# Attention and two feed-forward layers on one core: source order in the rounds, four slices decoded ahead, masks by the third unit

## The chip, the cores and the metric

One core of a Trainium2 chip runs the whole program. The metric is the device time of one execution in microseconds (us). TensorE (PE) multiplies, VectorE (DVE), ScalarE (ACT) and GpSimd (POOL) do the rest, SyncE (SP) issues nearly all loads and stores. Each engine works through its own queue in order and waits on semaphores of the others.

## What is computed

Sliding-window attention over 2 batches, 8 heads, 768 positions, head size 64 (window 128, 4 sink keys), then two feed-forward layers on the 1536 tokens of 512 values, with 2048 hidden values each:

```
scores = scale * q @ k.T, masked to (sink or window)
x = softmax(scores) @ v             -> 1536 x 512
g = where(h > 0, h, exp(min(h, 0)) - 1),  h = x @ w_in ;  x = g @ w_out
g = max(h, 0) + alpha * min(h, 0),        h = x @ w_in2 ; out = g @ w_out2
```

The weights arrive as 64-bit floating point numbers, and the kernel takes them apart itself on the chip.

## The kernel before

**Three products for one.** Every feed-forward product is made of three matmuls (`matmul3`, L287): each operand is split into a rounded part (wh, gh, xh) and a residual (wl, gl, xl).

**Decoding.** A half slice is 128 x 512 weights: slice fc of the first (io=0) or second matrix (io=1) of layer m. `load_w` (L192) brings its raw words over SP's queue. `decode_w` (L257) takes it apart in four phases, between which its caller can put other work: two activations on ScalarE (L266, L267), four steps on VectorE (L269 to L278), the cast wh on ScalarE (L282), the subtraction wl (L284) on VectorE, or on the engine that the caller names.

**Attention.** 32 units of one or two blocks of 110 queries, for two heads at a time. A loop over steps s (L610) runs three units at once: scores of unit s (L510, then per tile a fused mask and minimum on VectorE, L518, and an exponential on ScalarE, L523), the sums and their reciprocals (L533, L536) with the normalising on GpSimd (L540), the transposes of the probabilities of unit s-1 (L554) with copies out of PSUM (L638), and the product with the values of unit s-2 (L575), whose result is rounded on ScalarE (xh, L583) and its residual taken on VectorE (xl, L585). Masks are made on VectorE by `make_mask` (L454): blocks 0 and 1 ahead of the loop, 2, 3 and 4 at the end of steps 0, 1 and 5, from index ramps that GpSimd made at the start.

**Round 0 inside the attention.** While the attention runs, TensorE takes pieces of the first layer's round 0 as fill (L591): a round is four slices of hidden values, `g1` makes one slice's hidden values for a stretch of tokens, `g2` adds four slices' product to one quarter of the output. Where there is no fill, small matmuls keep TensorE busy (L246). The eight half slices of round 0 are decoded in steps 0 to 7, the first four with the subtraction on VectorE, the others on GpSimd. In this part (from L597) each engine's instructions stand in the order of the source.

**After a piece** (`after`, L316 and L353): for `g1` of layer 0 ScalarE's relu and exp (L321, L322), VectorE's combining step (L323), ScalarE's rounding copy gh (L335) and GpSimd's residual gl (L336); in the text this is the gate. For `g2` one copy (L355) or addition (L357). A PSUM slot (four of them) comes free when VectorE's or ScalarE's last read of it is done.

**The rounds.** The last stretch of round 0's tokens (328 columns, "the first item" in the text) and rounds 1 to 7 (each 24 pieces of 12 matmuls of 512 columns) follow in `mlp_rounds` (L393). Two sets of decoded weights alternate (`wa`, `wb`); the second lies in memory that the attention's buffers held. In the first item all eight half slices of round 1 are to be decoded, one at each piece; in a round k those of round k+1. Here the framework's scheduler orders the instructions of each engine by its own reckoning, and can also put those of the rounds ahead of the attention's where no buffer forbids it.

Of the kernel before, what the change touches and what calls it, by code (L numbers as in the profile page):

```python
# [21 lines left out]
P = 128  # L22
# [29 lines left out]

UB, SB, PB, LB = 2, 3, 5, 3

MS = {2: 0, 3: 1, 4: 5}

WPRE = 2


# [52 lines left out]
def attention_mlp2(  # L112
# [18 lines left out]
    wa = ctx.enter_context(tc.tile_pool(name="wa", bufs=FG))  # L131
    rawp = ctx.enter_context(tc.tile_pool(name="rawp", bufs=3))
    wdec = ctx.enter_context(tc.tile_pool(name="wdec", bufs=2))
# [39 lines left out]
    def load_v(g, pool=None):  # L173
        b, z, hp = sgs[g]
        n = VCH[z] * 2 * D
        if pool:
            t = pool.tile([P, max(VCH) * 2 * D], F32, tag="vr", name=f"vr{g}", bufs=LB)
# [191 lines left out]
    def done(steps):  # L369
        for _ in steps:  # L370
            pass

    def run(pieces):

        pend = []
        for p, extra in pieces:
            if p is None:
                done(pend.pop(0)())
                continue
            if extra:  # L380
                extra()
            pend.append(p())
            if len(pend) > 1:
                done(pend.pop(0)())
        for a in pend:
            done(a())

    def halves(k):

        m, r = divmod(k, NR)  # L390
        return [(m, r * FG + i, io) for io in range(2) for i in range(FG)] if k < 2 * NR else []

    def mlp_rounds(mlp, items, wpools):  # L393


        def g1(k, tok, i):
            m, r = divmod(k, NR)
            return mlp.g1(m, *tok[:2], r * FG + i)

        def g2(k, tok, d):  # L400
            m, r = divmod(k, NR)
            return mlp.g2(m, *tok[:2], r, d)


        todo = {it: [] for it in items}
        for k in range(2 * NR):
            of_round = [it for it in items if it[0] == k]
            hs = halves(k + 1)
            for j, h in enumerate(hs):
                todo[of_round[j * len(of_round) // len(hs)]].append((wpools[(k + 1) % 2], *h))  # L410
        order = [h for it in items for h in todo[it]]
        for h in order[:2]:
            load_w(*h[1:])
        state = {"at": 0}

        def weights_step():
            j = state["at"]
            if j + 2 < len(order):
                load_w(*order[j + 2][1:])
            done(decode_w(*order[j]))  # L420
            state["at"] = j + 1

        pieces, late = [], []
        for n, it in enumerate(items):
            mine = [lambda i=i, it=it: g1(*it, i) for i in range(FG)] + late
            late = [lambda d=d, it=it: g2(*it, d) for d in range(KC)]
            if n == 0:
                mine += [None] + late
                late = []
            step = len([p for p in mine if p]) // max(1, len(todo[it]))  # L430
            for j, p in enumerate(mine):
                if p is not None and todo[it] and j % step == 0:
                    todo[it].pop()
                    pieces.append((p, weights_step))
                else:
                    pieces.append((p, None))
        pieces += [(p, None) for p in late]
        run(pieces)

# [5 lines left out]

    def distance(blk):

        rel = relp.tile([P, KW[blk]], I32, tag=f"rel{blk}", name=f"rel{blk}")
# [28 lines left out]

    relp = ctx.enter_context(tc.tile_pool(name="relp", bufs=1))
    rels = {blk: distance(blk) for blk in MASKS}

# [3 lines left out]
    def fast_path():  # L484
        outer = ExitStack()
        ps_qk = outer.enter_context(tc.tile_pool(name="ps_qk", bufs=4, space=PSUM))
        ps = outer.enter_context(tc.tile_pool(name="ps", bufs=4, space=PSUM))
        inner = ExitStack()
        ga = inner.enter_context(tc.tile_pool(name="ga", bufs=FG + 1))
        at = inner.enter_context(tc.tile_pool(name="at", bufs=2))  # L490
        mlp = Mlp(ga, ps)
        soft, trans = {}, {}
        wraw.update(wfirst)

        def scores(i):
# [99 lines left out]


        order = inner.enter_context(tc.manual_schedule())  # L597
        make_mask(0)
        make_mask(1)
        ws = halves(0)  # L600
        for j in range(WPRE, WPRE + 3):
            load_w(*ws[j])
            if j < HP:
                load_v(j)
        for g in range(HP, HP + LB):
            load_kq(g, at)
            load_v(g, at)
        decodes = {}
        gates = []
        for s in range(nu + 2):  # L610
# [14 lines left out]
            if s == 0:  # L625
                decodes[0] = decode_w(wa, *ws[0], sub=nc.vector)
                next(decodes[0])
# [4 lines left out]
            if not take and s < nu:  # L632
                keep_busy(ps, "ps", BUSYN)
            if s < nu:
                normalised(s)
            if 1 <= s <= nu:
                for j, (out, in_) in enumerate(transposed(s - 1)):
                    (nc.scalar.copy if j and s < len(ws) else nc.vector.tensor_copy)(out, in_)  # L638
            if not take and s < nu:
# [9 lines left out]
            for blk, at_ in MS.items():  # L649
                if s == at_:  # L650
                    make_mask(blk)
            if s + 1 < len(ws):
                decodes[s + 1] = decode_w(wa, *ws[s + 1], sub=nc.vector if s + 1 < FG else nc.gpsimd)
                next(decodes[s + 1])
            if WPRE <= s and s + 3 < len(ws):
                load_w(*ws[s + 3])
            if s < nu:
# [3 lines left out]
            if s >= 2:  # L661
                g = units[s - 2][0]
                if s - 2 == last_of[g] and HP <= g and g + LB < len(sgs):
                    load_v(g + LB, at)
        for a in gates:
# [3 lines left out]
        inner.close()  # L669
        wb = outer.enter_context(tc.tile_pool(name="wb", bufs=FG))  # L670
        gb = outer.enter_context(tc.tile_pool(name="gb", bufs=2 * FG))
        mlp.gp = gb
        rounds = [(k, t) for k in range(1, 2 * NR) for t in TOK]
        mlp_rounds(mlp, [(0, TOK0[-1])] + rounds, (wa, wb))
        outer.close()

    def general_path():

        with ExitStack() as outer:
# [76 lines left out]
            mlp = Mlp(gb, ps)  # L756
            mlp_rounds(mlp, [(k, t) for k in range(2 * NR) for t in TOK], (wa, wb))

# [57 lines left out]
```

## Time and profile before

| | us |
|---|---|
| runs, median of 3 (lowest, highest) | 671.12 (671.01, 672.19) |
| profiled execution | 673.24 |
| its span | 671.1 |
| PE busy | 642.0 (96%) |
| DVE busy | 440.8 (66%) |
| ACT busy | 316.5 (47%) |
| POOL busy | 207.9 (31%) |

The profile is of one execution; its span runs from the first to the last instruction of the program, and the execution's own time includes what lies around it. Busy time of an engine counts its instructions, not its waiting; ends of matmuls are modelled, so a busy TensorE is not one at its peak. The time before an instruction in which its engine was idle is put down to what ended the wait.

### The profile page before, as it was taken

Reading aid. Unit: us, or ns where it says so; the run is one execution under the profiler, and the core shown is the slowest. Engines: PE = TensorE matmul, PEld = TensorE weight load, DVE = VectorE, ACT = ScalarE, POOL = GpSimd, SP = SyncE. Lnnn points to the kernel's source line nnn. Section 1 sums busy time; section 2 is a strip of 40 time slices with the busy share of each in tenths; the row PEclk is TensorE's granted clock in tenths of the full one; section 3 lists DMA queues with packets and bytes.
Section 4 is the critical chain, followed back from the end, with each engine's and each line's share of the span. In section 5 each row is a group of like instructions: output and inputs, shape, how many; then the busy total and the mean of one; then the engine's idle time right before and its main releaser. Section 6 shows DMA issues by size and latency. Waiting matters only on the chain.

```text
span 671.1 us, 9665 instructions
## 1 busy us (share of the span) xinstructions
PE 642.0 (96%) x3444; PEld 527.0 (79%) x3444; DVE 440.8 (66%) x925; ACT 316.5 (47%) x717; POOL 207.9 (31%) x257
## 2 busy tenths in 40 slices
PE   7966999999999899999999999999999999999996
PEld 6745888888877677888888888888888888888885
DVE  5798566756499997668465876694559673343332
ACT  5676476656478685547445733453524230110010
POOL 2346244534123322133205453332123311331130
PEclk8898899999999999999999999999999999999999
DMA  8665324620044242121112211221111000000112
GB/s 266 169 165 182 106 58 122 170 79 25 1 154 133 91 156 95 49 77 63 63 54 72 64 63 52 75 67 61 63 63 63 32 0 1 1 0 1 63 46 85
DMA packets 21659, 52.87 MB, mean 79 GB/s; under 512 B 2658, under 2 KB 9826, under 8 KB 21602
## 3 DMA queue, kind: packets, MB, share of 16 engines
q1 hardware_dynamic: 21024, 51.93, 24.8%
q8 instruction: 29, 0.48, 0.3%
q10 hardware_dynamic: 578, 0.24, 0.2%
q14 instruction: 28, 0.23, 0.1%
HBM read 49.01 MB, written 3.15 MB: 78 GB/s over the span
## 4 chain that ended last, share of the span: by engine, by line
PE 80%; DVE 11%; ACT 4%; issue 3%; POOL 1%; DMA 1%; ACTq 0%; DVEq 0%; POOLq 0%; SPq 0%
PE o L292 37%; PE h L292 34%; PE x L575 3%; PE t L554 2%; PE qk L510 2%; DVE wx L275 2%; ACT s L523 2%; DVE wl L284 1%; DVE wx L269 1%; DVE wx L278 1%; PE busy L250 1%; DVE u L323 1%; DVE pt L638 1%; DVE wx L272 1%; ACT wx L266 1%
## 5 line engine op out<-in xcount | busy, mean ns | idle before, releaser
L336 POOL TENSOR_TENSOR gl<-u,gh 128x512 fp32r<-128x512 f32 (+3 forms) x104 | 131.5, 1264 | 341.6 <-ACT gh L335 307.2
L292 PE MATMUL o<-gh,wh 128*128 128x512 f32 (+3 forms) x416 | 159.2, 383 | 3.7 <-DVE u L323 2.0
L292 PE MATMUL h<-xh,wh 128*128 128x512 f32 (+3 forms) x416 | 158.9, 382 | 0.0
L292 PE MATMUL o<-gl,wh 128*128 128x512 f32 (+3 forms) x416 | 157.2, 378 | 0.8 <-POOL gl L336 0.8
L292 PE MATMUL h<-xl,wh 128*128 128x512 f32 (+3 forms) x416 | 157.1, 378 | 0.0
L292 PE MATMUL h<-xh,wl 128*128 128x512 f32 (+3 forms) x416 | 156.9, 377 | 0.0
L292 PE MATMUL o<-gh,wl 128*128 128x512 f32 (+3 forms) x416 | 156.5, 377 | 0.0
L335 ACT CAST gh<-u 128x512 fp32r<-128x512 f32 (+3 forms) x104 | 61.0, 586 | 140.9 <-DVE u L331 118.9
L357 DVE TENSOR_TENSOR acc<-o,acc 128x512 f32<-128x512 f32 x72 | 49.4, 688 | 76.9 <-PE o L292 76.9
L292 PEld LDWEIGHTS o<-gh,wh 128*128 128x128 f32 x416 | 78.5, 189 | 23.2 <-DVE u L323 4.1
L292 PEld LDWEIGHTS h<-xh,wh 128*128 128x128 f32 x416 | 78.6, 189 | 17.1 <-DVE u L323 0.3
L292 PEld LDWEIGHTS o<-gl,wh 128*128 128x128 f32 x416 | 78.8, 189 | 15.9 <-POOL gl L336 1.8
L292 PEld LDWEIGHTS h<-xl,wh 128*128 128x128 f32 x416 | 78.7, 189 | 14.6
L292 PEld LDWEIGHTS h<-xh,wl 128*128 128x128 f32 x416 | 78.6, 189 | 14.7
L292 PEld LDWEIGHTS o<-gh,wl 128*128 128x128 f32 x416 | 78.7, 189 | 14.5
L540 POOL TENSOR_SCALAR s<-s,st 110x250 f32<-110x250 f32 (+5 forms) x112 | 52.7, 488 | 86.0 <-DVE st L536 42.6
L282 ACT CAST wh<-wx 128x512 fp32r<-128x512 f32 x64 | 39.5, 619 | 67.7 <-DVE wx L278 29.4
L327 DVE TENSOR_SCALAR u<-h,alpha_sb 128x512 f32<-128x512 f32 x48 | 35.9, 748 | 48.4 <-PE h L292 48.3
L523 ACT ACTIVATE s<-s,st 110x250 f32<-110x250 f32 (+5 forms) x112 | 53.1, 476 | 20.8 <-DVE st L518 20.8
L278 DVE CUSTOM_DVE_ANT_0 wx<-wx,wq 128x1024 uint16<-128x1024 uint16 x64 | 58.0, 906 | 1.3
L284 DVE TENSOR_TENSOR wl<-wx,wh 128x512 fp32r<-128x512 f32 x60 | 45.4, 759 | 17.6 <-PE o L292 9.2
L267 ACT ACTIVATE wq<-wr 128x512 int32<-128x512 uint32 x62 | 41.5, 669 | 32.9 <-DVE wx L278 29.4
(55 smaller groups left out, 664.3 us busy)
## 6 DMA issues: line engine op xcount, KB each, us to landing
wr<-in_w_dram SPq DMA_DIRECT2D x62, 512.0 KB, 3.5
kq<-in_kq_dram SPq DMA_DIRECT2D x16, 237.0 KB, 4.4
vr<-in_vc_dram SPq DMA_DIRECT2D x8, 384.0 KB, 3.7
out_dram<-acc SPq DMA_DIRECT2D x12, 256.0 KB, 2.0
kq<-in_kq_dram SPq DMA_DIRECT2D x16, 180.0 KB, 3.9
vr<-in_vc_dram SPq DMA_DIRECT2D x8, 256.0 KB, 4.0
acc<-in_w_dram SPq DMA_DIRECT2D x2, 512.0 KB, 5.4
kq<-in_kq_dram SPq DMA_DIRECT2D x8, 110.0 KB, 2.7
```

The source lines that it names most:

```text
L267: nc.scalar.activation(r, low.bitcast(U32), AF.Copy, scale=2.0**-29)
L278: nc.vector.tensor_tensor(out=x, in0=x, in1=r, op=ALU.add)
L282: nc.scalar.copy(wh, xf)
L284: (sub or nc.vector).tensor_tensor(out=wl, in0=xf, in1=wh, op=ALU.subtract)
L292: nc.tensor.matmul(out, a, c, start=(i == 0), stop=(i == n - 1))
L327: nc.vector.tensor_scalar(out=u, in0=hp, scalar1=0.0, scalar2=alpha_sb[:, fc : fc + 1], op0=ALU.min, op1=ALU.mult,)
L335: nc.scalar.copy(gh, u)
L336: nc.gpsimd.tensor_tensor(out=gl, in0=u, in1=gh, op=ALU.subtract)
L357: nc.vector.tensor_tensor(out=a, in0=po, in1=a, op=ALU.add)
L523: nc.scalar.activation(sb[:n, j, e, :w], sb[:n, j, e, :w], AF.Exp, bias=st[:n, 0, j, e : e + 1], scale=-1.0, accum_out=st[:n, 1, j, e : e ...
L540: nc.gpsimd.tensor_scalar(out=sb[:n, j, e, :w], in0=sb[:n, j, e, :w], scalar1=st[:n, 3, j, e : e + 1], scalar2=1.0, op0=ALU.mult, op1=ALU. ...
L575: nc.tensor.matmul(px[e * D : e * D + D, o : o + n], vr[:r, vs : vs + D], pt[:r, p0 : p0 + n], start=(k == 0), stop=(k == c - 1),)
```

## The change

1. The source's order holds on every engine for the rounds too (`manual_schedule` now encloses them). `mlp_rounds` is rewritten: the phases of a decode are dealt out over successive pieces (ScalarE's two activations at one piece, VectorE's four steps at the next, then the cast, then the subtraction), and a slice's load follows when the slice two before it is done.
2. Four of round 1's half slices (io=0) are decoded during the attention, in steps 19, 22, 25 and 28, into a pool `wb0` of their own; round 0's eight in steps 0, 1, 3, 4, 5, 6, 7 and 8. The first item decodes the other four, begun at its pieces 0, 2, 4 and 6.
3. All subtractions in the attention are on GpSimd.
4. The copies of the transposed probabilities stand ahead of the sums and the normalising; the second copy is on ScalarE in steps with a decode only.
5. Masks of blocks 2, 3 and 4 are made in steps 0, 1 and 2. Their index ramps lie in other buffers; those of blocks 3 and 4 are made inside the branch.
6. Buffers: raw slices 2 for 3, values 2 for 3, copied probabilities 4 for 5.

```diff
-UB, SB, PB, LB = 2, 3, 5, 3
-MS = {2: 0, 3: 1, 4: 5}
+UB, SB, PB, LB, VB = 2, 3, 4, 3, 2
+MS = {2: 0, 3: 1, 4: 2}
+DS = [0, 1, 3, 4, 5, 6, 7, 8, 19, 22, 25, 28]
...
-    rawp = ctx.enter_context(tc.tile_pool(name="rawp", bufs=3))
+    rawp = ctx.enter_context(tc.tile_pool(name="rawp", bufs=2))
...
-    def mlp_rounds(mlp, items, wpools):
+    def mlp_rounds(mlp, items, wpool, early=0):
...
+        pieces, late, order = [], [], []
         for n, it in enumerate(items):
             mine = [lambda i=i, it=it: g1(*it, i) for i in range(FG)] + late
             late = [lambda d=d, it=it: g2(*it, d) for d in range(KC)]
             if n == 0:
-                mine += [None] + late
+                mine += late
                 late = []
+            pieces += [[p, None, n == 0 and j == FG, it[0]] for j, p in enumerate(mine)]
+        for k in range(2 * NR):
+            mine = [p for p in pieces if p[3] == k]
+            hs = halves(k + 1)[early if k == items[0][0] else 0 :]
+            for j, h in enumerate(hs):
+                mine[j * len(mine) // len(hs)][1] = h
+            order += hs
+        pieces += [[p, None, False, None] for p in late]
+        for h in order[:2]:
+            load_w(*h)
+        active, after = [], None
+        for p, h, wait, _ in pieces:
+            for gen, nxt in list(active):
+                if next(gen, active) is active:
+                    active.remove((gen, nxt))
+                    if nxt:
+                        load_w(*nxt)
+            if h:
+                i = order.index(h)
+                active.append((decode_w(wpool(h), *h), order[i + 2] if i + 2 < len(order) else None))
+                next(active[-1][0])
+            if wait:
+                done(after())
+                after = None
+            now = p()
+            if after:
+                done(after())
+            after = now
+        done(after())
...
+        outer.enter_context(tc.manual_schedule())
+        wb0 = outer.enter_context(tc.tile_pool(name="wb0", bufs=FG))
...
+        rels.update({blk: distance(blk, at) for blk in MASKS[3:]})
...
-        order = inner.enter_context(tc.manual_schedule())
         make_mask(0)
         make_mask(1)
-        ws = halves(0)
-        for j in range(WPRE, WPRE + 3):
+        ws = halves(0) + halves(1)[: len(DS) - 2 * FG]
+        for j in range(WPRE, HP):
             load_w(*ws[j])
-            if j < HP:
-                load_v(j)
+            load_v(j)
...
             if s == 0:
-                decodes[0] = decode_w(wa, *ws[0], sub=nc.vector)
+                decodes[0] = decode_w(wa, *ws[0], sub=nc.gpsimd)
...
+            if 1 <= s <= nu:
+                for j, (out, in_) in enumerate(transposed(s - 1)):
+                    (nc.scalar.copy if j and s in decodes else nc.vector.tensor_copy)(out, in_)
             if s < nu:
                 normalised(s)
-            if 1 <= s <= nu:
-                for j, (out, in_) in enumerate(transposed(s - 1)):
-                    (nc.scalar.copy if j and s < len(ws) else nc.vector.tensor_copy)(out, in_)
...
-            if s + 1 < len(ws):
-                decodes[s + 1] = decode_w(wa, *ws[s + 1], sub=nc.vector if s + 1 < FG else nc.gpsimd)
+            if s + 1 in DS:
+                i = DS.index(s + 1)
+                decodes[s + 1] = decode_w(wb0 if i >= 2 * FG else wa, *ws[i], sub=nc.gpsimd)
                 next(decodes[s + 1])
-            if WPRE <= s and s + 3 < len(ws):
-                load_w(*ws[s + 3])
+            if s in DS and WPRE <= DS.index(s) + 2 < len(ws) and DS.index(s) >= WPRE:
+                load_w(*ws[DS.index(s) + 2])
...
-        wb = outer.enter_context(tc.tile_pool(name="wb", bufs=FG))
+        wb1 = outer.enter_context(tc.tile_pool(name="wb1", bufs=FG))
```

## Rows read from the trace of the kernel before

**Rows 1.** The page, part 1: engines' busy us and share of the span
```profile
PE 642.0 (96%) x3444; PEld 527.0 (79%) x3444; DVE 440.8 (66%) x925; ACT 316.5 (47%) x717; POOL 207.9 (31%) x257
```

**Rows 2.** Busy time by stretch: stretch, us, each engine's busy us, PEclk, DMA share, GB/s
```profile
106.00:179.00 73.00, 71.70 (x590) 60.32 (x590) 43.97 (x173) 43.26 (x144) 29.83 (x57) 1.00 0.31 84
...
179.00:196.60 17.60, 16.13 (x105) 14.68 (x106) 15.81 (x27) 13.55 (x29) 3.62 (x4) 1.00 0.28 96
...
196.60:267.60 71.00, 68.27 (x289) 53.44 (x289) 65.89 (x101) 50.94 (x92) 18.46 (x13) 1.00 0.38 125
...
267.60:334.00 66.40, 66.40 (x290) 54.07 (x289) 43.27 (x65) 36.47 (x64) 18.17 (x13) 1.00 0.20 64
```

**Rows 3.** Timeline, VectorE at 55 us: start, us, engine, line, operation, out<-in
```profile
55.18 0.42 DVE L269 TENSOR_SCALAR wx<-wx 128x512 f32<-128x512 f32 x1
```

**Rows 4.** Timeline, 37 to 43 us, GpSimd and VectorE
```profile
37.59 1.28 POOL L284 TENSOR_TENSOR wl<-wx,wh 128x512 fp32r<-128x512 f32 x1
...
37.90 1.26 DVE L269 TENSOR_SCALAR wx<-wx 128x512 f32<-128x512 f32 x1
...
42.67 2.61 DVE L463 SCALAR_TENSOR_TENSOR mask<-skey,lims,mask 128x6 f32<-128x6 int32 x1
```

**Rows 5.** Timeline, first score steps of units 5 and 6, scores of unit 10
```profile
35.80 0.41 DVE L518 CUSTOM_DVE_ANT_0 s<-qk,mask 110x250 f32<-110x250 f32 x1
...
45.21 0.41 DVE L518 CUSTOM_DVE_ANT_0 s<-qk,mask 110x250 f32<-110x250 f32 x1
...
73.18 1.11 PE L510 MATMUL qk<-kq 64*110 64x256 f32 x8
```

**Rows 6.** Timeline, 50 to 53 us, GpSimd
```profile
50.12 1.82 POOL L540 TENSOR_SCALAR s<-s,st 110x250 f32<-110x250 f32 x4 [4.86 <-ACT wq L267]
...
51.91 0.65 POOL L336 TENSOR_TENSOR gl<-u,gh 128x220 fp32r<-128x220 f32 x1
```

**Rows 7.** Timeline, 114 to 116 us, a gate of 328 columns
```profile
114.27 0.48 ACT L322 ACTIVATE u<-u 128x328 f32<-128x328 f32 x1
...
114.90 0.48 DVE L323 SCALAR_TENSOR_TENSOR u<-u,h 128x328 f32<-128x328 f32 x1
...
115.42 0.47 ACT L335 CAST gh<-u 128x328 fp32r<-128x328 f32 x1 [0.67 <-DVE u L323]
```

**Rows 8.** Timeline, first item: its first matmul and its fourth residual
```profile
179.40 0.42 PE L292 MATMUL h<-xh,wh 128*128 128x328 f32 x1
...
192.49 0.94 POOL L336 TENSOR_TENSOR gl<-u,gh 128x328 fp32r<-128x328 f32 x1 [1.71 <-ACT gh L335]
```

**Rows 9.** Timeline, 8 to 13 us, a decode on ScalarE and VectorE
```profile
8.77 0.65 ACT L266 ACTIVATE wx<-acc 128x512 f32<-128x512 f32 x1
...
9.32 0.65 ACT L267 ACTIVATE wq<-acc 128x512 int32<-128x512 uint32 x1
...
11.20 0.69 DVE L278 CUSTOM_DVE_ANT_0 wx<-wx,wq 128x1024 uint16<-128x1024 uint16 x1
...
11.93 0.62 ACT L282 CAST wh<-wx 128x512 fp32r<-128x512 f32 x1 [0.74 <-DVE wx L278]
...
12.67 0.68 DVE L284 TENSOR_TENSOR wl<-wx,wh 128x512 fp32r<-128x512 f32 x1
```

**Rows 10.** Busy time by stretch, 47 to 54 us
```profile
47.40:50.40 3.00, 0.00 (x0) 0.00 (x0) 2.86 (x8) 2.97 (x9) 0.28 (x1) 1.00 0.14 31
...
50.50:53.70 3.20, 3.20 (x23) 2.93 (x24) 2.62 (x11) 2.86 (x11) 3.20 (x6) 0.51 0.96 272
```

**Rows 11.** Busy time by stretch, 80 to 98 us
```profile
80.00:98.00 18.00, 17.46 (x169) 14.58 (x169) 12.13 (x53) 12.39 (x46) 8.98 (x18) 1.00 0.30 83
```

**Rows 12.** Timeline, 112 to 116 us, a residual product and the next values
```profile
112.79 0.39 DVE L585 TENSOR_TENSOR xl<-x,xh 128x220 fp32r<-128x220 f32 x1 [0.51 <-ACT xh L583]
...
115.28 0.84 PE L575 MATMUL x<-pt,vr 110*64 110x110 f32 x12
```

**Rows 13.** The page, part 6: loads of raw slices, us to landing
```profile
wr<-in_w_dram SPq DMA_DIRECT2D x62, 512.0 KB, 3.5
```

More of the change, by code (lines that the diff above doesn't have):

```diff
@@ L176, in load_v @@
         if pool:
-            t = pool.tile([P, max(VCH) * 2 * D], F32, tag="vr", name=f"vr{g}", bufs=LB)
+            t = pool.tile([P, max(VCH) * 2 * D], F32, tag="vr", name=f"vr{g}", bufs=VB)
         else:
@@ L371, in done @@
             pass
[L373 to L386, printed above, removed]
     def halves(k):
@@ L402, in g2 @@
             return mlp.g2(m, *tok[:2], r, d)
[L405 to L423, printed above, removed]
+        pieces, late, order = [], [], []
         for n, it in enumerate(items):
@@ L427, in mlp_rounds @@
             if n == 0:
-                mine += [None] + late
+                mine += late
                 late = []
[L430 to L438, printed above, removed]
+            pieces += [[p, None, n == 0 and j == FG, it[0]] for j, p in enumerate(mine)]
[27 more added lines that the diff above has]
+        done(after())
     skey = const.tile([P, SINK], I32, tag="skey", name="skey")
@@ L444, in attention_mlp2, with distance @@
     masks = {}
-    def distance(blk):
-        rel = relp.tile([P, KW[blk]], I32, tag=f"rel{blk}", name=f"rel{blk}")
+    def distance(blk, pool=None):
+        if pool:
+            rel = pool.tile([P, 4 * QB], F32, tag="pt", name=f"rel{blk}", bufs=PB).bitcast(I32)
+        else:
+            o = HP * (2 * KTOT[0] + VCH[0] * 2 * D) + WPRE * 2 * DM + sum(KW[i] for i in MASKS if i < blk)
+            rel = room[:, o : o + KW[blk]].bitcast(I32)
+        rel = rel[:, : KW[blk]]
         for c, n, k in mask_runs(blk):
@@ L476, in attention_mlp2 @@
     mask_t = const.tile([P, sum(KW[i] for i in MASKS)], F32, tag="mask", name="mask")
-    relp = ctx.enter_context(tc.tile_pool(name="relp", bufs=1))
-    rels = {blk: distance(blk) for blk in MASKS}
+    rels = {blk: distance(blk) for blk in MASKS[:3]}
     alpha_sb = const.tile([P, NFC], F32, tag="alpha", name="alpha_sb")
@@ L594, in fast_path @@
             fill += [(at_, lambda c0=c0, n=n, d=d: mlp.g2(0, c0, n, 0, d)) for d in range(KC)]
-        order = inner.enter_context(tc.manual_schedule())
         make_mask(0)
         make_mask(1)
-        ws = halves(0)
-        for j in range(WPRE, WPRE + 3):
+        ws = halves(0) + halves(1)[: len(DS) - 2 * FG]
+        for j in range(WPRE, HP):
             load_w(*ws[j])
-            if j < HP:
-                load_v(j)
+            load_v(j)
         for g in range(HP, HP + LB):
             load_kq(g, at)
-            load_v(g, at)
+            if g < HP + VB:
+                load_v(g, at)
         decodes = {}
@@ L662, in fast_path @@
                 g = units[s - 2][0]
-                if s - 2 == last_of[g] and HP <= g and g + LB < len(sgs):
-                    load_v(g + LB, at)
+                if s - 2 == last_of[g] and HP <= g and g + VB < len(sgs):
+                    load_v(g + VB, at)
         for a in gates:
@@ L673, in fast_path, with wpool @@
         rounds = [(k, t) for k in range(1, 2 * NR) for t in TOK]
-        mlp_rounds(mlp, [(0, TOK0[-1])] + rounds, (wa, wb))
+        def wpool(h):
+            m, fc, io = h
+            return wa if (m * NR + fc // FG) % 2 == 0 else (wb0, wb1)[io]
+        mlp_rounds(mlp, [(0, TOK0[-1])] + rounds, wpool, len(ws) - 2 * FG)
         outer.close()
@@ L756, in general_path @@
             mlp = Mlp(gb, ps)
-            mlp_rounds(mlp, [(k, t) for k in range(2 * NR) for t in TOK], (wa, wb))
+            mlp_rounds(
+                mlp, [(k, t) for k in range(2 * NR) for t in TOK],
+                lambda h: (wa, wb)[(h[0] * NR + h[1] // FG) % 2],
+            )
     fast = nc.values_load(flag_i[0:1, 0:1], min_val=0, max_val=1)
```

## The prediction

> **What bounds the kernel now.** I read the page first, then the busy time by stretch, then the timelines of the stretches in which TensorE is not full. TensorE is busy 96% of the span [rows 1], so only what it waits for can be won. By stretch [rows 2], the third of the four (round 1) takes 71.0 us, the last (round 2) 66.4 us for the same 288 matmuls of 512 columns. VectorE shows why: 65.89 of 71.0 us busy in round 1 against 43.27 of 66.4 in round 2, because the rounds' weights are decoded as early as buffers allow, and the gate steps that make TensorE's operands queue behind them. From round 2 on TensorE is dense to the end: nothing in the change can make that part shorter. The first item, from 179.40 [rows 8] to 196.6, takes 17.2 us; its 96 matmuls of 328 columns come to 14.1 at the rate of round 2 (66.4 / 288 x 328 / 512 = 0.148 each), eight pieces of 1.77.
>
> Earlier, at 55.18 us, a decode of round 1 begins on VectorE between two steps of round 0's last decode, in the middle of the attention [rows 3]: the framework's scheduler pulled it out of the rounds, and a second one follows. And [rows 4] while GpSimd subtracts a decoded slice (37.59 to 38.87), VectorE's first decode step takes 1.26 us, where the one at 55.18, with GpSimd idle, takes 0.42 [rows 3]; a mask step on six columns takes 2.61 us behind two such subtractions. The two-input operation of GpSimd holds VectorE up until it ends. From unit 18 on TensorE is nearly full through the attention: 71.70 of 73.0 us in the first stretch of [rows 2].
>
> **The change, part by part.** The sum is made against the profiled span, 671.1 us; that execution took 673.24, the median run 671.12, so a difference of spans is put on the median.
>
> *Round 1 in source order.* A round holds eight decodes in 24 pieces, one begun every third piece, as round 2 has them on average. It should run as round 2 does: 66.4 for 71.0, **-4.6 us**. It begins with eight gate pieces in a row, which ScalarE and VectorE work through more slowly than TensorE makes them; four PSUM slots take that up, as I count just barely (see the slower rival). Bounds 0 and -4.7.
>
> *The first item.* Four decodes A to D start at its pieces 0, 2, 4 and 6, and the order on ScalarE and VectorE is now fixed: cast of A, both activations of B, then the gate of piece 1; four steps of B, then the gate of piece 2; cast of B, activations of C, then the gate of piece 3. So decode and gate, ScalarE and VectorE, alternate in one chain. Its prices: two activations 1.2 (8.77 to 9.97), the four VectorE steps 2.4 (from the end of the first activation, 9.42, to 11.89), cast 0.6, subtraction 0.7 [rows 9]; relu and exp 0.95, the combining step 0.5, the rounding copy 0.47 [rows 7]; GpSimd's residual 0.94 [rows 8]. From the first matmul: activations of A end at 1.6 and its VectorE steps at 3.3; gate of piece 0 to 4.3; cast of A 4.9; activations of B 6.1; gate of piece 1 to 7.5; subtraction of A and the residual of piece 1 to 9.1; steps of B to 11.4; gate of piece 2 to 12.3; cast of B and activations of C to 14.1; gate of piece 3 to 16.0; its residual 16.9. Piece 4 cannot end before that, and TensorE is in order, so pieces 5 to 7 follow: 16.9 + 0.3 + 5.3 = 22.5. TensorE is nearly idle from 7 to 17 us of it. When it had been idle from 47.4 to 50.4, its granted clock was 0.51 in the 3.2 us that followed [rows 10], the lower of its two levels of 1.2 and 2.4 GHz; half the work of 3.2 us is 1.6, and I add 1.2, since here it is not wholly idle. 23.7 against 17.2: **+6.5 us**. Now the residual of piece 3 starts 13.1 us after the first matmul (192.49 less 179.40, [rows 8]), with the scheduler interleaving single steps. Bounds 0 and +7.5.
>
> *The first ten units.* Three things happen. The pulled-forward decodes are gone. The mask of block 4 moves from unit 5 to unit 2, where no subtraction waits, so its 2.61 us [rows 4] become some 0.3. The subtraction of every slice goes to GpSimd: three more of 1.27 us there for three of 0.68 on VectorE [rows 9]. In a step with a decode VectorE's round is then, from the end of the sums: GpSimd normalises 1.82, takes the residual 0.65 [rows 6], subtracts 1.28 [rows 4], which with the hand-over is 3.9; VectorE's first decode step, ready at 2.4 (scores, ScalarE's exponentials and cast, residual product), ends 0.3 after that; its other three steps 1.8, the copy and the sums 0.9 make 6.9, with the hand-overs 7.0. Without a residual, as from unit 5 to 6, it is 0.65 less, but the first fill's combining step 0.4 more: 6.75. The score steps of units 5 and 6 start at 35.80 and 45.21 now [rows 5]. After: 35.1 (one decode less up to there and no mask later, but two collisions), 41.85, then three rounds of 7.0, so that unit 9 starts at 62.85. The fill's last weights are now decoded one unit later, at unit 8, so at unit 9 TensorE waits for GpSimd's subtraction until 66.6 and the scores of unit 10 start at 69.6 instead of 73.18 [rows 5]: **-3.6 us**. Bounds: -9, if nothing collides, and 0.
>
> The Trainium skill (Perfetto Trace Analysis, section Optimizing Scalar/DVE Operations) says that with VectorE saturated some work may be offloaded, even to GpSimd. By that alone the three moved subtractions would give back 2 us of VectorE time. The row of 1.26 us says that each costs VectorE about 0.83, more than the 0.68 it saves.
>
> *Copies ahead of the sums.* The transposed probabilities are now copied before the sums and reciprocals. Where TensorE's fill is short, it is idle for 0.54 us of 18 [rows 11], partly behind such copies; over units 10 to 17 I take **-0.5**, between 0 and -1.
>
> *Four decodes at units 19, 22, 25, 28.* At unit 19 the residual product's step ends VectorE's work at 113.2 and TensorE wants the copied probabilities at 115.28 [rows 12]. With the copies first, the sums come about 0.5 us later than now, so the decode runs from 113.5, held by a residual on GpSimd to 115.9, the copy ends at 116.3: 1.07 late. The same count gives 0.9 at unit 22 and 1.35 at unit 28, and nothing at unit 25, whose step is longer because two pieces of fill lie in it. 3.3, of which TensorE's idle 1.3 us in this stretch [rows 2] takes some: **+2.8**. Bounds 0 and +4.6. ScalarE's five extra operations and GpSimd's subtraction lie beside TensorE's work there.
>
> *The rest.* The raw slices have two buffers for three, the values two for three. On SP's queue a slice's load now waits for VectorE's third step of the slice two before it, about one step ahead of its use, and the keys' and values' loads queue behind it; a step is 5 to 7 us early on and a load lands in 3.5 [rows 13], so I cost it at nothing; without that cover it would be up to 1 us a step. Eight index ramps on GpSimd move behind the branch, ahead of its first normalising, where it idled: nothing. The one buffer less for copied probabilities: nothing, each is read a unit before it is needed again.
>
> Sum: -4.6 + 6.5 - 3.6 - 0.5 + 2.8 = +0.6, **671.7 us**. A measurement of this kernel tells about 0.2% (1.34 us) from no change.
>
> **The rivals.** *Nothing collides (faster).* If VectorE's decode steps meet no subtraction on GpSimd, the rounds of units 4 to 8 lose the 0.95 (twice) and 1.35 (three times) that they wait in the sum: 6 us, **665.7**. For it: GpSimd has a slack of 2 us or more in each step, and a cast that comes earlier would let it subtract before it normalises. Against: the order on GpSimd puts each subtraction behind the normalising and right ahead of VectorE's step. This is also what the Trainium skill's offloading sentence, cited above, would lead to. *The first item interleaves (faster).* If the residual of piece 3 came as early as now (14.0), the item would take 20.8 with the clock, 2.9 less: **668.8**. For it speaks only that the work is the same; the fixed order speaks against.
>
> *Round 1's eight gate pieces (slower).* A piece costs ScalarE and VectorE in turn 2.7 us, three of them with a decode 10.6, against 8.3 on TensorE. By my count the slot that the third `g2` piece behind the eight needs comes free 0.3 us before TensorE wants it. Decides: if a piece costs 0.3 more, for instance because each decode step meets a 1.3-us residual, the eighth is 2.4 us later, TensorE waits 2.1 us in this round, and its next pieces start behind: with the bound of the late decodes, **674.5 to 676**. *The rounds keep the scheduler's order.* Then round 1 and the first item stay and the sum is -1.3: 669.8.
>
> **How the numbers follow.** Forecast 0.36, of which 0.24 within 0.2%, 0.05 below and 0.07 above; no collisions 0.25; interleaved first item 0.10; round 1's backlog 0.26; scheduler's order 0.03, just within. Faster 0.40, same 0.27, slower 0.33. The range leaves about a tenth out at either side: below, the first rival with a microsecond more, above, the backlog with the late decodes at their bound: 664.8 to 676.0. Cases of both signs hold most of the chance; the likeliest one's own range is 669.5 to 674.
>
> **What would show it.** Right: round 1 at 66.4 us with VectorE some 45 us busy; no decode of the rounds ahead of unit 19; the first item near 23 us with TensorE waiting for a residual or a combining step, and its matmuls at half speed after; first decode steps near 1.3 us in units 4 to 8; scores of unit 10 near 69.6. Wrong: a first item of 17 us or less, a round 1 over 68, or first decode steps of 0.43 in units 4 to 8.

## The result, and the profile after

The changed kernel takes **676.53 us** (median of 20 runs, 672.05 to 679.09) against 671.36 for the kernel before on the same chips (20 runs, 670.0 to 673.39): ratio 1.0067, 95% interval 1.0051 to 1.0083, slower by some 4.5 us. The profiled execution has a span of 677.0 us for 671.1. First the page's busy times after, which answer to [rows 1]:

```profile
PE 637.3 (94%) x3444; PEld 528.3 (78%) x3444; DVE 450.8 (67%) x914; ACT 316.8 (47%) x720; POOL 214.3 (32%) x265
```

TensorE is busy 4.7 us less with the same matmuls, and the span is 5.9 us longer. The products stand in the same order too, but for the second half of the first item, where the framework's scheduler had interleaved three `g2` pieces. Where the time went shows by stretch (stretch, us, each engine's busy us, PEclk, DMA share, GB/s), cut where the same work begins: the scores of unit 19, the first item, round 1, round 2, the end. A step of a unit is, in what follows, the time from its scores on TensorE to the next unit's. Two stretches of the kernel before, then four of the changed one:

```profile
110.15:179.40 69.25, 67.95 (x557) 57.10 (x556) 41.88 (x162) 40.47 (x133) 28.92 (x55) 1.00 0.30 80
...
267.64:665.76 398.12, 398.12 (x1729) 324.15 (x1727) 238.19 (x353) 141.62 (x241) 112.13 (x83) 1.00 0.14 49
```

```profile
104.93:184.99 80.06, 70.12 (x557) 58.62 (x556) 48.10 (x177) 48.55 (x148) 34.25 (x60) 0.98 0.35 98
184.99:209.26 24.27, 18.90 (x98) 17.09 (x97) 14.38 (x26) 14.19 (x30) 3.98 (x4) 0.79 0.27 86
209.26:277.94 68.68, 66.04 (x290) 53.84 (x289) 44.29 (x68) 39.77 (x71) 17.38 (x14) 1.00 0.21 70
277.94:671.63 393.69, 393.24 (x1729) 323.79 (x1727) 270.20 (x376) 147.51 (x255) 112.58 (x83) 1.00 0.17 57
```

And the scores of unit 10, which stand at 73.18 in [rows 5]:

```profile
67.21 1.11 PE L509 MATMUL qk<-kq 64*110 64x256 f32 x8
```

Against the prediction's terms, in us:

| stretch | before | after | difference | predicted |
|---|---|---|---|---|
| to the scores of unit 10 | 73.18 | 67.21 | -6.0 | -3.6 |
| units 10 to 18 | 36.97 | 37.72 | +0.8 | -0.5 |
| units 19 to 31 | 69.25 | 80.06 | +10.8 | +2.8 |
| first item | 17.20 | 24.27 | +7.1 | +6.5 |
| round 1 | 71.04 | 68.68 | -2.4 | -4.6 |
| rounds 2 to 7 | 398.12 | 393.69 | -4.4 | 0 |

Two rows are surprises: units 19 to 31 lose 8 us more than counted, and rounds 2 to 7, of which the prediction says that "nothing in the change can make that part shorter", are shorter. For the first, the waits of SyncE's queue between 90 and 182 us of the changed kernel, TensorE's between 104 and 185 us (engine, line, what it waited for: us, times, longest), and SyncE's timeline (start, us, instruction):

```profile
SPq L198 <- DVE wx L278: 34.3, 3, 20.0
...
PE x L574 <- DMA vr<-in_vc_dram: 5.5, 2, 2.9
```

```profile
103.05 0.54 SPq L183 DMA_DIRECT2D vr<-in_vc_dram  x1
110.07 0.33 SPq L198 DMA_DIRECT2D wr<-in_w_dram  x1
110.50 1.25 SPq L171 DMA_DIRECT2D kq<-in_kq_dram  x2
111.86 0.53 SPq L183 DMA_DIRECT2D vr<-in_vc_dram  x1
```

The load of a raw slice (`wr`) waits for VectorE's third decode step (L278 of the changed kernel) to give up one of the two raw buffers, and the keys and values behind it wait with it. TensorE's value products (L574) then wait for the values, 5.5 us in all. After the second of these waits TensorE's granted clock is at the lower of its two levels:

```profile
137.55:140.97 3.42, 3.42 (x15) 3.42 (x14) 0.39 (x1) 1.46 (x7) 0.00 (x0) 0.50 0.35 116
```

3.4 us of work at half speed are 1.7 us more.

### The profile page after: what moved, and what is told of

It is laid out like the page before. It is cut to its first block, busy times and chain, and to the rows that moved or that the text cites. A ratio compares the mean times of both kernels' runs of the same rounds, so it can differ in the third digit from the quotient of the medians.

```text
span 677.0 us, 9674 instructions
## 1 busy us (share of the span) xinstructions
PE 637.3 (94%) x3444; PEld 528.3 (78%) x3444; DVE 450.8 (67%) x914; ACT 316.8 (47%) x720; POOL 214.3 (32%) x265
## 4 chain that ended last, share of the span: by engine, by line
PE 69%; DVE 16%; ACT 8%; DMA 3%; issue 3%; POOL 1%; DVEq 0%; ACTq 0%; POOLq 0%
PE o L295 33%; PE h L295 29%; DVE wx L278 3%; PE x L574 3%; DMA vr<-in_vc_dram 3%; DVE wx L275 3%; DVE u L326 2%; DVE wx L272 2%; PE t L553 2%; DVE wx L281 2%; ACT s L522 1%; DVE pt L633 1%; ACT u L325 1%; PE qk L509 1%; ACT u L324 1%
## 5 line engine op out<-in xcount | busy, mean ns | idle before, releaser
L339 POOL TENSOR_TENSOR gl<-u,gh 128x512 fp32r<-128x512 f32 (+3 forms) x104 | 129.9, 1249 | 327.6 <-ACT gh L338 326.9
L295 PE MATMUL h<-xh,wh 128*128 128x512 f32 (+3 forms) x416 | 157.3, 378 | 0.2 <-DVE acc L360 0.2
L295 PE MATMUL h<-xl,wh 128*128 128x512 f32 (+3 forms) x416 | 155.5, 374 | 0.1
L295 PEld LDWEIGHTS o<-gh,wh 128*128 128x128 f32 x416 | 80.2, 193 | 25.3 <-ACT gh L338 4.6
L295 PEld LDWEIGHTS o<-gl,wh 128*128 128x128 f32 x416 | 80.3, 193 | 18.3 <-POOL gl L339 5.3
L539 POOL TENSOR_SCALAR s<-s,st 110x250 f32<-110x250 f32 (+5 forms) x112 | 49.0, 456 | 97.8 <-DVE st L535 52.9
L326 DVE SCALAR_TENSOR_TENSOR u<-u,h 128x512 f32<-128x512 f32 (+3 forms) x56 | 33.7, 602 | 65.4 <-ACT u L325 65.4
L278 DVE SCALAR_TENSOR_TENSOR wx<-wr,wx 128x512 int32<-128x512 int32 x62 | 64.5, 1040 | 2.1
L287 DVE TENSOR_TENSOR wl<-wx,wh 128x512 fp32r<-128x512 f32 x52 | 47.2, 908 | 11.3 <-ACT wh L285 11.3
```

The costliest lines, as they stand in the source:

```text
L278: nc.vector.scalar_tensor_tensor(out=x, in0=high, scalar=-0x40000000, in1=x, op0=ALU.bitwise_and, op1=ALU.bitwise_or)
L287: (sub or nc.vector).tensor_tensor(out=wl, in0=xf, in1=wh, op=ALU.subtract)
L295: nc.tensor.matmul(out, a, c, start=(i == 0), stop=(i == n - 1))
L326: nc.vector.scalar_tensor_tensor(out=u, in0=u, scalar=1.0, in1=hp, op0=ALU.subtract, op1=ALU.max)
L339: nc.gpsimd.tensor_tensor(out=gl, in0=u, in1=gh, op=ALU.subtract)
L539: nc.gpsimd.tensor_scalar(out=sb[:n, j, e, :w], in0=sb[:n, j, e, :w], scalar1=st[:n, 3, j, e : e + 1], scalar2=1.0, op0=ALU.mult, op1=ALU. ...
```

## The experiments

**Where the rounds' 4.4 us come from.** In the kernel before, the 48 matmuls of four pieces take 11.20 us in some groups of four and 10.91 in others, as in these two neighbours:

```profile
289.46:300.66 11.20, 11.20 (x50) 9.00 (x48) 5.48 (x7) 3.62 (x7) 4.07 (x3) 1.00 0.23 79
300.66:311.57 10.91, 10.91 (x49) 9.01 (x48) 7.36 (x12) 6.73 (x13) 1.30 (x1) 1.00 0.14 49
```

Slow are the second weight pool against the activations and the first pool against the gates. In the changed kernel every group takes 10.88, but for 1.8 us of stalls around the start of layer two. By the sizes of the program's tiles there is one difference: the activations and the first pool start 1248 bytes past a multiple of 2048 in both kernels, the second pool and the gates 1536 bytes past one before and 1248 after. The change took away the pool of index ramps: five ramps rounded up to 32 bytes are 448 + 896 + 1024 + 992 + 1024 = 4384 = 2 x 2048 + 288 bytes. The first run gives the kernel before the same alignment:

```
 relp = ctx.enter_context(tc.tile_pool(name="relp", bufs=1))
+nc.gpsimd.memset(relp.tile([P, 440], F32, tag="pad", name="pad")[:, :1], 0.0)
```

> The kernel before, with 1760 bytes of empty tile behind the index ramps, so that the rounds' tiles (weights and gates) lie 1248 bytes past a multiple of 2048, as the activations and the first weight pool do, instead of 1536. Theory (address): the 512-column pieces that take 2.80 us in the kernel before (every second group of four: weights from the second pool against the activations, weights from the first pool against the gates) fall to 2.72 us; from 267.64 us on 144 pieces at 2.72 are about 392 for 398.1, and round 1 gives up to 1 us more: 664.5 to 666.5 us. Rival (the source order on the engines makes the pieces shorter): nothing changes, 671 us, still 2.80 in the same groups.

Measured: **665.34 us**, ratio 0.9906 (0.9878 to 0.9934). The rounds from 2 on, and a group that took 11.20:

```profile
266.69:658.53 391.84, 391.84 (x1729) 324.14 (x1727) 238.04 (x353) 141.59 (x241) 112.05 (x83) 1.00 0.15 50
288.45:299.33 10.88, 10.88 (x49) 9.01 (x48) 5.48 (x7) 3.63 (x7) 4.06 (x3) 1.00 0.25 88
```

398.12 became 391.84; round 1 stayed at 71.06, where VectorE is busy for 65.94 us. Then the reverse: empty tiles of 32, 64 and 256 bytes ahead of the second pool of the changed kernel.

```
+padp = outer.enter_context(tc.tile_pool(name="padp", bufs=1))
+nc.gpsimd.memset(padp.tile([P, 8], F32, tag="pad", name="pad")[:, :1], 0.0)
 outer.enter_context(tc.manual_schedule())
```

> The changed kernel with 32 bytes of empty tile ahead of the second weight pool: its tiles and the gates then lie 32 bytes off the activations and the first pool. Theory (address, with a unit above 32 bytes): half the groups of four pieces go to 2.80 us again, and the time rises by some 6 us to 683. If the unit is 32 bytes or less, or the rival (source order) holds: 2.72 everywhere, 677 us.

> As with 32 bytes, but 64 bytes of empty tile. If the operands' addresses matter modulo 64 bytes: all pieces at 2.72 us, 677. If they matter modulo more (128, 2048): half the groups at 2.80 again, 682 us. Judged by the pieces, not by the total.

> 256 bytes of empty tile ahead of the second weight pool. If the operands' addresses matter modulo 256 or 128: 2.72 us in all groups. If modulo 512 or more: 2.80 or 2.75 in the groups that were so with 64 bytes.

Measured: 682.15, 679.81 and 682.22 us (one run each; in the last units 19 to 31 took 83.0 us, so the groups decide and not the totals). The first four pieces of round 1, activations against the second pool, at 32, 64 and 256 bytes:

```profile
206.53:217.73 11.20, 11.20 (x51) 9.02 (x50) 5.42 (x10) 7.19 (x13) 2.42 (x2) 1.00 0.18 61
```

```profile
205.36:216.56 11.20, 11.20 (x50) 9.03 (x49) 5.41 (x10) 7.16 (x13) 2.42 (x2) 1.00 0.18 64
```

```profile
212.58:223.48 10.90, 10.90 (x50) 9.01 (x49) 5.18 (x10) 6.98 (x13) 2.17 (x2) 1.00 0.14 50
```

32 bytes bring the pattern of the kernel before back (11.20 / 48 = 233 ns a matmul against 10.88 / 48 = 227), 64 bytes too, some gate groups at 11.01 instead; 256 bytes do not. The source order, the same in all four, has no part in it. So what counts is how the stationary and the moving operand of a matmul lie to each other, and a difference of 256 bytes counts as none: the 288 bytes of the kernel before are 256 and 32.

**Units 19 to 31.** Three raw buffers again, then three value buffers instead:

```
-rawp = ctx.enter_context(tc.tile_pool(name="rawp", bufs=2))
+rawp = ctx.enter_context(tc.tile_pool(name="rawp", bufs=3))
```

```
-UB, SB, PB, LB, VB = 2, 3, 4, 3, 2
+UB, SB, PB, LB, VB = 2, 3, 4, 3, 3
```

> The changed kernel with three buffers for raw slices again, nothing else. Theory (SyncE's queue): the loads of the last two late slices, issued in the steps of units 19 and 22, no longer wait for VectorE's third decode step, the key and value loads behind them go out 5 us earlier, and the value products no longer wait for them: units 19 to 31 take 72 to 73 us for 80.1, the whole 669 to 670. Rival 1 (two value buffers alone make the values late): under 2 us less. Rival 2 (the late decodes' work on VectorE and GpSimd costs the time): no change.

> The changed kernel with three buffers for values again, two for raw slices: the other half of what was taken from the queue. Theory (the wait on SyncE's queue costs only because the values have no group to spare): with a load issued one group earlier the values are there in spite of the 5 us that a slice's load holds the queue, units 19 to 31 take 72 to 74 us as with three raw buffers, the whole 669 to 671. Rival (the held queue makes the keys late as well, or the raw slice itself): units 19 to 31 stay above 76 us, the whole above 673.

Measured: **669.96 us**, ratio 0.9974 (0.9961 to 0.9988), and **669.87**, ratio 0.9975 (0.9961 to 0.9988). The stretch, and with three raw buffers TensorE's waits in it:

```profile
102.41:175.30 72.89, 68.47 (x557) 57.04 (x556) 48.11 (x177) 48.19 (x148) 34.29 (x60) 1.00 0.41 115
```

```profile
PE x L574 <- DVE pt L633: 3.3, 5, 1.0
PE o L295 <- POOL gl L339: 1.0, 2, 0.6
```

```profile
104.23:177.14 72.91, 68.49 (x558) 57.05 (x557) 48.11 (x177) 48.20 (x148) 34.28 (x60) 1.00 0.38 105
```

7.2 us go, 5.5 of waits and 1.7 of the lower clock, and no value product waits for a load any more. With three raw buffers the slice's load goes out at once, and the next value load 2.3 us after the scores of unit 19 start (102.41) instead of 6.9 us after them (104.93 in the changed kernel):

```profile
101.18 0.37 SPq L198 DMA_DIRECT2D wr<-in_w_dram  x1
103.30 1.25 SPq L171 DMA_DIRECT2D kq<-in_kq_dram  x2
104.66 0.53 SPq L183 DMA_DIRECT2D vr<-in_vc_dram  x1
```

Either buffer suffices: the held queue costs nothing while the values have a group to spare. The change took both away together. The price varies: in the five profiles with this order and both buffers cut (the changed kernel, the three with empty tiles, and the one with listed pieces below) units 19 to 31 take 77.5 to 83.0 us, in the four with one of them back 72.9 to 73.0.

**The first item and round 1.** The decodes at listed pieces, and piece 3's gate ahead of the decode steps of piece 4 (`begin`: 4, 6, 9, 12, 16, 18, 21, 24, then every third piece):

```
+        for h, j in zip(order, begin):
+            pieces[j][1] = h
...
         for p, h, wait, _ in pieces:
+            if wait:
+                done(after())
+                after = None
             for gen, nxt in list(active):
...
-            if wait:
-                done(after())
-                after = None
             now = p()
```

> The changed kernel with the rounds' decodes begun at listed pieces: the four of the first item at its pieces 4 and 6 and at pieces 9 and 12, those of round 1 from piece 16 on, all others at every third piece; and the gate of piece 3 written ahead of the decode steps of piece 4. Theory (the chain of alternating decode and gate, then a backlog of eight gate pieces): the first item falls from 24.3 to 17 or 18 us, the stalls of 1.5 and 1.7 us in round 1's second and third layer-2 pieces go: 24.3 + 68.7 becomes 17.5 + 65.5, the whole 667. Rival (the clock's lower level and the amount of work, not the order, make the item long): the item stays above 21 us. Rival for the backlog (the eight gate pieces alone, without decodes, overrun the PSUM slots): the item falls, round 1 stays near 68.5, the whole 670.

Measured: **665.17 us**, ratio 0.9906 (0.9879 to 0.9933). First item and round 1:

```profile
182.48:199.28 16.80, 15.47 (x98) 14.71 (x97) 7.42 (x14) 9.49 (x21) 3.57 (x4) 1.00 0.10 31
199.28:265.41 66.13, 65.85 (x291) 53.91 (x289) 40.10 (x61) 38.69 (x68) 16.83 (x13) 1.00 0.21 64
```

Both theories hold. The stalls around the start of layer two went as well: the rounds from 2 on take 391.84 us here. That it was the chain is seen in the changed kernel on GpSimd, whose four residuals wait each for a gate behind a decode, and in a run with the two moved lines alone (and three raw buffers):

```profile
189.44 0.90 POOL L339 TENSOR_TENSOR gl<-u,gh 128x328 fp32r<-128x328 f32 x1 [7.96 <-ACT gh L338]
193.00 1.09 POOL L339 TENSOR_TENSOR gl<-u,gh 128x328 fp32r<-128x328 f32 x1 [2.65 <-ACT gh L338]
196.81 0.89 POOL L339 TENSOR_TENSOR gl<-u,gh 128x328 fp32r<-128x328 f32 x1 [2.72 <-ACT gh L338]
200.38 1.09 POOL L339 TENSOR_TENSOR gl<-u,gh 128x328 fp32r<-128x328 f32 x1 [2.68 <-ACT gh L338]
```

> Three raw buffers, and of the cure of the rounds only the two moved lines: the gate of piece 3 written ahead of the decode steps of piece 4; the decodes stay where they were. Theory (the chain as the prediction counted it): of its terms only the cast of B and the two activations of C, 1.8 us, leave the path to piece 3's residual: first item 25.1 (with three raw buffers) to 23.3 us. Rival (piece 3's gate alone is held, the rest runs beside): 18 us or less.

Measured: 670.5 us (one run); the item took 177.91 to 200.57, 22.7 us for 25.1. TensorE's waits in the item of the changed kernel, then of this run:

```profile
PE o L295 <- ACT gh L338: 3.8, 2, 2.1
PE o L295 <- POOL gl L339: 1.6, 3, 0.7
```

```profile
PE o L295 <- ACT gh L338: 2.1, 1, 2.1
PE o L295 <- POOL gl L339: 1.6, 3, 0.7
```

One wait of 1.7 us has gone, the rest is as it was. The fourth residual shows it without the clock's part:

```profile
191.68 0.89 POOL L339 TENSOR_TENSOR gl<-u,gh 128x328 fp32r<-128x328 f32 x1 [1.07 <-ACT gh L338]
```

It starts 13.8 us after the item's first matmul, for 15.3 to 15.4 in all seven profiles with the old order: 1.6 us for the 1.8 that were counted. The item's own length is a coarser measure; with the old order it lies between 23.7 and 25.1 us.

**Who subtracts.** On top of three raw buffers, `sub=nc.vector` for the slices decoded in the attention.

> The changed kernel with three raw buffers and with the subtraction of every slice decoded in the attention on VectorE instead of GpSimd; beside the run with three raw buffers alone (span 668.1). Theory (a two-input GpSimd operation holds VectorE: 0.95 us lost on a decode step for 0.69 saved): rounds of units 6 to 8 as long or 0.3 us shorter each, the whole -2 to +0.5 us. Rival (the offloaded work is free, nothing collides): VectorE has 12 times 0.69 us more in steps that it bounds, the whole +3 to +6 us.

Measured: 671.84 us, ratio 0.9987 (0.9969 to 1.0006) beside 0.9974 (0.9961 to 0.9988) with three raw buffers alone: the intervals overlap. Units 19 to 31, with four of the twelve slices, take 73.33 for 72.89. The four subtractions are 2.7 us more VectorE work and cost 0.4; so neither expectation fits. The collision itself is settled. With the subtraction on VectorE the second decode step takes 0.43 us in every unit from 3 to 8, as in the first row, and with it on GpSimd 1.38 in units 6 to 8, as in the second (the changed kernel):

```profile
45.46 0.43 DVE L275 TENSOR_SCALAR wx<-wx 128x512 int32<-128x512 int32 x1
```

```profile
42.72 1.38 DVE L275 TENSOR_SCALAR wx<-wx 128x512 int32<-128x512 int32 x1
```

Over all the profiles here this step takes 0.41 to 0.43 us where GpSimd has nothing under way, and 1.37 or 1.38 each of the 35 times that it meets GpSimd's subtraction of a decoded slice. But in this one profile to be rid of it gains nothing: from unit 5's first score step on VectorE to unit 9's it is 28.0 us, and 26.3 to 27.6 in the ten with the subtraction on GpSimd in the same order. What it does to the whole early part stays open: in this run the step of unit 2 took 7.0 us at a granted clock of 0.55, and 4.6 at 0.94 with three raw buffers alone.

**Both cures, then two sizes.** Three raw buffers and listed pieces together; then the late decodes at other units (`DS` ends in 10, 17, 25, 31); then also the sums ahead of the copies again:

```
+            if s < nu:
+                normalised(s)
             if 1 <= s <= nu:
                 for j, (out, in_) in enumerate(transposed(s - 1)):
                     (nc.scalar.copy if j and s in decodes else nc.vector.tensor_copy)(out, in_)
-            if s < nu:
-                normalised(s)
```

> Both cures together: three raw buffers, and the rounds' decodes at listed pieces with the gate of piece 3 written ahead. The places are disjoint in time (units 9 to 31; first item and rounds), so theory: the gains add, 662.7 - 2.5 - 7.3 is a span of 653, a time of 655 us, faster than either kernel. Rival (the late value loads had hidden something, or the rounds wait for loads next): 658 or more.

> Both cures, and the four late decodes at units 10, 17, 25 and 31 instead of 19, 22, 25 and 28: at 10, 17 and 25 two pieces of fill stand in one step, 31 is the last unit. Theory (a late decode costs what VectorE is late beyond TensorE's fill: 1.0, 1.0 and 1.6 us at the steps of 19, 22 and 28, nothing at 25): scores of unit 10 to the first item 110.7 to about 107.5 us, the time 657. Rival (the decode costs the same wherever it stands, by the engine's total): 110.7 stays, 660.

> As raw3_rounds_slots (span 656.5), with the sums and the normalising written ahead of the copies of the transposed probabilities again, as before the change. Theory (copies first cost: the sums come 0.74 us later, GpSimd normalises and takes the fourth gate's residual later, and TensorE waits for it at units 15, 22 and 29): the steps of 15, 22 and 29 go from 4.93, 5.38 and 5.60 back to 4.2, 4.8 and 4.9, up to -2 us, less what the steps with a decode lose by later copies (0 to 1): 655 to 656.5 in time, a span of 654.5 to 655.5. Rival (the prediction's: the copies bound, copies first gains 0.5): those three steps stay, the rest lose 0.5 to 1: a span of 657 or more.

Measured: **659.83** us, ratio 0.9833 (0.979 to 0.9875); **658.33**, 0.9784 (0.9758 to 0.9811); **656.06**, 0.9774 (0.9749 to 0.9798). The first misses its theory by 5 us and lies where the rival put it, though not for the rival's reason: no load is late. The 2.5 us that were counted for the early part were chance. The run with listed pieces alone had the scores of unit 10 at 65.11, not at the changed kernel's 67.21, and this one has them at 66.51: +1.4 for -2.5. Units 19 to 31 gave 6.7 (79.66 to 72.97) for 7.3. All three kernels hold the 6 us of the addresses, as the changed kernel does; beside the kernel before with the same alignment (665.34) they still gain 5.5, 7.0 and 9.3 us. From the scores of unit 10 to the first item the three take 177.20 - 66.51 = 110.7, 109.4 and 107.8 us. TensorE's waits from 65 to 180 us, late decodes moved, then with the sums first as well:

```profile
PE o L297 <- POOL gl L341: 2.0, 3, 1.0
PE x L579 <- DVE pt L638: 1.8, 2, 1.0
```

```profile
PE x L579 <- DVE pt L640: 2.7, 4, 1.1
PE o L297 <- POOL gl L341: 0.3, 1, 0.3
```

Moving the decodes gave 1.3 us where 3.2 was expected. From one unit's scores to the next, the step of 20 fell from 5.43 to 4.39 and that of 23 from 5.19 to 4.78, but the one of 22 stayed at 5.4, though its decode was gone, and the new places cost 0.3 (10) and 0.7 (31). With the sums first the steps of 15, 22 and 29 go from 4.93, 5.38 and 5.60 to 4.19, 4.78 and 4.90. That was the copies' doing: GpSimd normalises after the sums and takes the gate's residual after that, which TensorE's next piece needs. The other way round the copies come later, and the steps of 11 and 13 rise from 3.47 and 3.64 to 3.89 and 3.97; with 0.3 that the step of 10 gets back, 1.6 us remain. The timeline at unit 15, whose scores start at 86.11 with the copies first and 87.32 with the sums first:

```profile
89.12 0.65 POOL L341 TENSOR_TENSOR gl<-u,gh 128x220 fp32r<-128x220 f32 x1
```

```profile
89.58 0.65 POOL L341 TENSOR_TENSOR gl<-u,gh 128x220 fp32r<-128x220 f32 x1
```

3.0 us against 2.3 into the step.

## Why the prediction was right or wrong

The time lies a little above the range (676.0) by the median of the runs, inside it by the ratio (671.12 x 1.0067 = 675.6). "Slower" had 0.33, less than "faster". That the time is near the range's end and not beyond it is luck: 8 us were lost at a step costed at nothing, and 4.4 were won where no gain was thought possible. Step by step:

- **First item, right.** +7.1 for +6.5, by the chain as counted: the fourth residual starts 200.38 - 184.99 = 15.4 us after the first matmul, for 16.0 predicted and 13.1 before [rows 8]. Two more terms stand behind that residual. The lower clock cost 2.1 us (4.3 us behind the residual at a granted clock of 0.50) for the 1.2 that were added. And TensorE's order was part of the loss: before, the scheduler had let it begin three `g2` pieces with the slices that were ready, as these rows of the kernel before show (three first matmuls, `gh` with `wh`, ahead of a `gl`), and only 3.2 us were left when the fourth residual ended; now 7.8, of which 5.7 without the clock. The prediction has this in "TensorE is in order, so pieces 5 to 7 follow", but names the chain alone.

```profile
189.26 0.42 PE L292 MATMUL o<-gh,wh 128*128 128x328 f32 x1 [0.72 <-DVE u L323]
189.87 0.57 PE L292 MATMUL o<-gh,wh 128*128 128x328 f32 x2 [0.19 <-ACT gh L335]
190.28 0.31 PE L292 MATMUL o<-gl,wh 128*128 128x328 f32 x1
```

- **The rest, the step that failed.** "A step is 5 to 7 us early on and a load lands in 3.5, so I cost it at nothing" looked at the slice's own load alone. The wait was named with what is queued behind it, and not followed to the value load, which has two buffers at the same time. It cost 7.2 of the 80.06 us of units 19 to 31; the bound of 1 us a step came in two large waits instead. In the early part a value load was late by 3.0 us as well, at 59.7, in the changed kernel's profile, and by 3.3 in the one with 32 bytes, but in none of the others.
- **Late decodes, mechanism right.** Without the late values the stretch loses 3.6 (72.89 - 69.25). The steps of 20, 23 and 29 gave back 1.0, 0.4 and 0.9 when their decodes moved, for 1.07, 0.9 and 1.35 predicted at units 19, 22 and 28: 2.3 us for the 2.8 of the sum. Unit 25's costs nothing, as said (its step is 6.78 us before and 6.78 after). The other 1.3 us of the 3.6 belong to the copies.
- **Copies ahead of the sums, wrong sign.** -0.5 predicted; +0.75 at unit 15 and +0.6 and +0.7 at 22 and 29, and no other step of units 10 to 18 changed by more than 0.04. The prediction saw the copies that TensorE waits for and not the sums, behind which GpSimd's residual stands.
- **First ten units, mis-sized.** -6.0 for -3.6; in ten profiles with the same early order the scores of unit 10 start between 64.7 and 67.6. VectorE's rounds, counted at 6.75 and 7.0 us, took 6.51, 6.62, 6.60 and 6.60; its first score step of unit 5 starts at 33.42 for 35.1, that of unit 9 at 59.75 for 62.85. From there to the scores of unit 10 it took 7.5 for 6.75, with a late value load in it where the prediction had a subtraction. The collision is there: beside GpSimd's subtraction the first decode step takes 1.23 and 1.49 us in units 4 and 5, and in units 6 to 8, where the subtraction starts later, the second one 1.38 (the row above, which answers to [rows 4]). The subtraction beside it:

```profile
42.34 1.47 POOL L287 TENSOR_TENSOR wl<-wx,wh 128x512 fp32r<-128x512 f32 x1
```

  How much of the 6.0 us each of the three causes brought was not separated.
- **Round 1, rival.** -4.6 predicted, -2.4 measured. The slower rival's mechanism is what happened, and a round 1 over 68 us was named as a sign of being wrong: the second and third `g2` pieces behind the eight gate pieces took 4.23 and 4.42 us to the start of the next one, for 2.72, 3.2 in all, while that next one waited for a gate's combining step to give up its slot:

```profile
PE o L295 <- DVE u L326: 2.6, 2, 1.4
```

  The count also spread eight decodes over 24 pieces; round 1 has 20. With the decodes spread and begun behind the gate pieces it took 66.13, the 66.4 of the prediction and a little less.
- **Rounds 2 to 7, not foreseen.** Taken at nothing, -4.4: 6.3 by the address, less 1.8 us of stalls around the start of layer two. With equal addresses the change's own work is slower by much more: 676.5 against 665.3 us, medians of the runs.

By its terms the prediction is 0.6 and the profile 5.9: +8.0 at units 19 to 31, +2.2 in round 1, +1.3 at units 10 to 18 and +0.6 in the first item, against -2.4 in the early part and -4.4 in the rounds.

By the Trainium skill (Perfetto Trace Analysis, section Optimizing Scalar/DVE Operations), work may be offloaded from a saturated VectorE even to GpSimd. Late in the attention, where VectorE is busy for 48 of 73 us and so not saturated, the trace agrees weakly: 2.7 us of VectorE work saved are worth 0.4 us. The section's own warning, that the two share a read port and the move might not help, fits the row of 1.38 us.

## What to carry to other kernels

Whoever removes a buffer asks who stands behind the load that now waits, on the queue that issues it, and how many buffers those have; a wait that is harmless alone cost 7 us here because two margins were cut at once. In a source order over several engines the order within a step is a chain: write ahead what another engine's next step needs (the gate before the decode, the sums before the copies), and spread side work evenly. Compare matmul durations of equal shapes by operand pair before and after any change of allocation.

## What was unexpected of the hardware

A matmul of 512 columns follows the one before it after 227 ns or after 233 ns, at the same granted clock of 1.00, depending on how its stationary and its moving tile lie to each other: alike modulo 256 bytes 227, 32 or 64 bytes apart 233 (some pairs at 64 bytes 229). What in the memory makes it so, and which offsets between 64 and 256 are good, stays open. It is worth 6 us here. By the Trainium skill (SBUF — State Buffer, section SBUF: two separate sides) contention comes at the port that VectorE and GpSimd share and at the DMA ports alone. The 2.9% here (11.20 against 10.88 us) went with the addresses of TensorE's own operands, with the same work on the other engines; the measurement decides.

In the early part the profiles of one and the same order differ by up to 3 us. The steps of units 7 and 8 with three raw buffers, for 6.62 and 6.60 in the changed kernel:

```profile
41.55:48.16 6.61, 4.38 (x46) 3.64 (x45) 6.10 (x18) 5.53 (x16) 3.86 (x7) 1.00 0.72 196
48.16:57.58 9.42, 7.22 (x45) 6.20 (x44) 8.85 (x21) 5.55 (x16) 4.85 (x7) 0.66 0.47 130
...
51.40:57.60 6.20, 6.14 (x38) 5.60 (x38) 5.70 (x18) 2.78 (x11) 3.86 (x6) 0.50 0.42 137
```

After 2.2 us in which TensorE was idle (to 51.46) the granted clock is 0.50, the lower of the two levels of 1.2 and 2.4 GHz, and the step takes 9.42 us. In other runs it is the step of unit 7 or that of unit 9 that the lower clock lengthens. Terms of less than 3 us in this part can't be read from one profile.
